# Converting 64-bit weights on the chip: nine landing places, two VectorE steps instead of three, and another order of work

## The chip, the cores and the metric

One NeuronCore of a Trainium2 chip runs the whole program. The metric is the device time of one execution in microseconds (us), lower is better. The engines are TensorE (PE, with PEld for its weight loads), VectorE (DVE), ScalarE (ACT), GpSimd (POOL) and SyncE (SP, which only issues DMAs here). Each runs its own queue of instructions strictly in order and waits on semaphores for the others.

## What is computed

A block-sparse attention over 4 batches, 8 heads, 768 positions and head size 64, followed by a feed-forward layer on its output:

```python
def _attn_ref(q, k, v, sampled_blocks):      # blocks of 32 positions, 24 blocks
    scores = scale * np.matmul(q, k.transpose(0, 1, 3, 2))
    mask = np.abs(blk_i - blk_j) <= window   # neighbours, first and last block, 3 sampled blocks
    ...
    attn = softmax(np.where(mask, scores, -1e9))
    return np.matmul(attn, v)

def _moe_ref(x, w_in, w_out):                # x (3072,512), w_in (512,2048), w_out (2048,512)
    h = x @ w_in
    g = h * np.clip(h + 3.0, 0.0, 6.0) / 6.0
    return g @ w_out
```

The weights arrive as 64-bit floats, and are made into 32-bit ones on the chip.

## The kernel before

**Tiling.** The attention is cut into 24 units, u0 to u23: a batch and a group of four blocks of queries (128 rows). Three units make a chunk of 384 rows, and each of the eight chunks goes through 16 feed-forward steps (m0 to m15 for the first chunk, m127 is the last of all). A step takes one column block of `w_in` and one row block of `w_out`: weights w0, w1 for step 0, w2, w3 for step 1 and so on to w31. Only the first chunk meets weights that are not yet on the chip as 32-bit floats. From m16 on they lie in the SBUF tiles `win` and `wout` (16 slices of 512 columns each).

**A unit.** `s` (two halves) makes the scores, `r_` (DVE, eight of them) adds the bias and takes the minimum, `e` (ACT, eight) the exponential, `t` (PE) turns them, `c` (DVE or ACT) copies them out of PSUM, `a` (PE) multiplies by the values, `n_` (DVE) divides, `x` (PE) turns the result, and `xh`, `xl` split it into a high and a low part of reduced precision. The units of a batch's group 0 (u3, u9, u15, u21) have two quarters like the others and a second part (`gs`, `gr`, `ge`, `gt`, `gc`, `ga`, ...) for the two blocks that see all keys. Values come by plain DMAs (`values`, issued by SP) and, for the sampled blocks, by indirect DMAs (`gather`, issued by POOL), into a ring `VR` of six places.

**A step.** `h` is 12 matmuls, three `o` of three matmuls each; between them ACT (`ga`, `gh`) and DVE (`gb`, and `gl` on DVE or POOL) make the activation and split it. In front of each step, `hi` (ACT) and `lo` (DVE or POOL) split the two weights. `oc` and `od` copy the result out and send it to HBM.

**A weight.** `load` brings 512 KB of raw words (low and high word of each number side by side) into a buffer `wraw`, of which there are two. `size` (ACT) scales the high word, read as a float, by 2^-112 into the weight's slice of `win` or `wout`; `bits0` (DVE) shifts that left by three; `bits1` (DVE) shifts the low word right by 29 and joins it; `bits2` (DVE) joins the sign. Then `hi` and `lo` follow. A raw buffer is free for the next load when `bits2` has read it.

**The order** is written out by hand in the table `SCORE`: a list of phrases such as `w2 size; u1 a gather0`, read from front to back, each of which records an operation (a suffix .d, .a, .p names the engine where there is a choice). Every engine's queue is this list, cut down to its own operations.

All operations are recorded by one helper, so that the profile gives them one line (L235); they are told apart by their tiles.

Of the kernel before, what the change touches and what calls it, by code (L numbers as in the profile page):

```python
# [28 lines left out]
MASKED = -8000000000.0  # L29

# [10 lines left out]
k0 load keys0; u0 q values0 values1 values2 values3; k0 clamp flag; u1 q; u0 near0.d near1.a; k0 spread; u1 values0; u0 near2.d near3.a chosen0.p; u1  # L41
values1; u0 ends0.d; w0 load; u0 ends1.d ends2.d; w1 load; u0 chosen1.p ends3.d; k0 bias number; u1 near0.d near1.a; k0 place; u0 chosen2.p; k0 rows;
u1 ends0.d ends1.d; u0 chosen3.p gather0 s0 gather1 s1 r_00 e00 r_01 e01 r_02 gather2; u2 q; u0 r_10; u1 near2.a; u0 t00 r_03 e02 gather3 r_11 e03
c00.d e10 t01; u1 chosen0.p; u0 e11 r_12; w0 size; u0 c01.d t10 e12; u1 chosen1.p; u0 r_13; w1 size; u0 c10.d e13; u1 near3.d chosen2.p; u2 near0.d
near1.a; u0 t11 d c11.a; u1 chosen3.p; w0 bits0; w1 bits0; w0 bits1; u0 a; u1 gather0; w1 bits1; u1 gather1; w0 bits2; u1 s0 values2; u0 n_; u1
values3; w0 hi; u2 chosen0.p values0; w1 bits2; u0 x; u2 values1; u1 s1; w2 load; u0 xh; u1 r_00; u2 chosen1.p; w3 load; w1 hi; w0 lo.d; u3 q; u1 e00
r_01; w1 lo.p; u1 r_10; u2 near2.a; u1 r_02 e01 gather2 r_11 e10 t00 r_03 e02 r_12 e03 gather3 c00.d e11 t01 e12 r_13 t10; u2 chosen2.p; u1 c01.d; u2
near3.a; u1 e13 c10.d; w2 size; u2 chosen3.p; u1 t11 d c11.a; u3 near2.d; u2 gather0; u3 near3.d; w3 size; u0 xl; w2 bits0; u2 gather1 s0; w3 bits0;
w2 bits1; u3 chosen2.p; u2 s1 r_00; w2 bits2; u2 e00; u1 a; u4 q; u3 chosen3.p; u2 r_01; u4 near0.a; w4 load; u2 r_10; w2 hi; u4 chosen0.p; u2 r_02
e01 values2; u1 n_; u2 e02 t00 values3; w2 lo.p; u3 values2; u2 r_03 e10; u1 x; u3 values3; u2 r_11 c00.a; w3 bits1; u2 e03; u4 near1.p; u2 e11 t01  # L50
r_12; u4 chosen1.p; u1 xh; u2 t10 c01.d; u3 s0; u2 e12 r_13 c10.a gather2; u1 xl; u2 e13; w3 bits2; w4 size; u2 t11 gather3 c11.d; w3 hi; w5 load; u2
d; u4 near2.a; u3 z0; w4 bits0; u4 near3.a; w3 lo.d; u3 gather2 r_00; w4 bits1; u3 e00 gather3; u2 a; u3 r_01; w4 bits2; u4 chosen2.p; u3 e01 r_02; w6
# [28 lines left out]
a; m13 gl.p; w27 hi; w29 load; w27 lo.d; u7 values2; u6 n_; m13 o0; u7 values3; w28 size; u8 values0; u6 x; m13 o1; w28 bits0; m13 o2; w28 bits1; u8
keys0; u7 s0; w28 bits2 hi; u7 r_00 e00 r_01; w28 lo.p; w30 load; w29 size; u7 r_02 r_03 e01; u8 values1; u7 gather2; m14 h; w29 bits0; u7 e02; w29
bits1; u7 e03 gather3; w29 bits2; m14 ga; u8 gather0; w31 load; w29 hi; m14 gb; u8 keys1; w29 lo.d; m14 gh gl.p; w30 size; m14 o0; u8 gather1; w30
bits0 bits1; m14 o1; w30 bits2; m14 o2; w30 hi; w0 hi; w30 lo.d; w0 lo.p; m15 h; w31 size bits0; m16 h; w31 bits1; m15 ga; w2 hi; m15 gb; u6 xh; w2
lo.p; w31 bits2; m15 gh; u6 xl; w31 hi; m15 gl.p; m17 h; m16 ga; w31 lo.d; w1 hi; m16 gb; w4 hi; w1 lo.p; m16 gh; m15 o0; w4 lo.d; m17 ga; u7 s1; m16
# [131 lines left out]
def fused_kernel(ctx: ExitStack, tc, qT, kN, kS, kB, vS, vB, picks, sampled, sampled_t, placing, cand, spread, w_in, w_out, ident_d, out):  # L217
# [564 lines left out]
```

## Time and profile before

| | |
|---|---|
| median of three runs | 804.61 us (802.95 to 804.74) |
| the profiled execution: time, span | 808.03 us, 806.2 us |
| PE busy | 764.5 us (95% of the span) |
| DVE, ACT, POOL busy | 508.8, 458.1, 334.1 us |
| DMA | 114.57 MB |
| mean granted TensorE clock | 0.982 |

The span runs from the program's first instruction to its last; the time has a little around it (1.8 us here). "Busy" of PE counts matmuls whose ends are modelled, so a stretch in which PE is 100% busy need not be PE at its peak. A group of instructions is told as engine, operation, what it writes <- what it reads.

### The profile page before, as it was taken

To read this page: it belongs to the slowest core of one execution; us is meant where nothing else is said; L and a number is where in the kernel's file an instruction comes from. 1 tells how busy PE (TensorE), PEld (TensorE's weight loads), DVE (VectorE), ACT (ScalarE), POOL (GpSimd) and SP (SyncE) were. 2 spreads that over 40 slices of the span, in tenths; PEclk is the share of its full clock that TensorE was granted. 3 is DMA by queue.
4 is the path that set the end of the run, shared out by engine and by line. 5 is a ranking of instruction groups with operands and counts; after the bars stand their busy time and mean duration, and the time that the engine had idled before them with its cause. 6 is when DMAs were issued, how large, how long until landed. Compare 5 with 4: busy or idle time off the path is not lost.

```text
span 806.2 us, 22075 instructions
## 1 busy us (share of the span) xinstructions
PE 764.5 (95%) x8662; PEld 635.7 (79%) x8662; DVE 508.8 (63%) x1173; ACT 458.1 (57%) x1113; POOL 334.1 (41%) x344
## 2 busy tenths in 40 slices
PE   5879888879999999999999999999999999999996
PEld 3568666658888888888888888888888788888995
DVE  5888788776556665566566764565566765555452
ACT  4674666546545766546555656556645657455453
POOL 5864363355334434445442434445443334321231
PEclk9899899999999999999999999999999999999998
DMA  8785379884123540766543540666444420311001
GB/s 307 230 253 165 119 229 322 274 297 127 30 93 93 180 139 2 244 206 188 143 134 93 170 150 2 202 203 218 139 122 122 151 91 1 120 48 39 1 1 40
DMA packets 73271, 114.57 MB, mean 142 GB/s; under 512 B 9139, under 2 KB 40759, under 8 KB 73167
## 3 DMA queue, kind: packets, MB, share of 16 engines
q1 hardware_dynamic: 65858, 89.95, 34.9%
q0 software_dynamic: 7040, 23.07, 9.3%
q8 instruction: 68, 1.11, 0.6%
q14 instruction: 37, 0.30, 0.1%
q10 hardware_dynamic: 268, 0.14, 0.1%
HBM read 106.84 MB, written 6.29 MB: 140 GB/s over the span
## 4 chain that ended last, share of the span: by engine, by line
PE 77%; DVE 1%; ACT 1%; issue 0%; DMA 0%; POOL 0%; POOLq 0%; SPq 0%; ACTq 0%
PE out L235 31%; PE h L235 30%; PE att L235 17%; DVE win L235 1%; DMA out_dram<-ot 0%; ACT p L235 0%; POOL wlo_in L235 0%; ACT whi_in L235 0%; ACT g L235 0%; DVE pt L235 0%; ACT whi_out L235 0%; ACT ot L235 0%; POOLq L778 0%; DVE wlo_out L235 0%; SPq L235 0%
## 5 line engine op out<-in xcount | busy, mean ns | idle before, releaser
L235 PE MATMUL h<-x,whi_in 128*128 128x384 f32 x1024 | 264.7, 339 | 1.6 <-ACT whi_in L235 1.6
L235 PEld LDWEIGHTS h<-x,whi_in 128*128 128x128 f32 x1024 | 186.8, 189 | 15.3 <-issue 2.9
L235 ACT ACTIVATE g<-h,half_b 128x384 f32<-128x384 f32 x128 | 74.4, 581 | 176.9 <-PE h L235 172.5
L235 PE MATMUL h<-x,wlo_in 128*128 128x384 f32 x512 | 173.1, 338 | 1.6 <-POOL wlo_in L235 1.4
L235 DVE SCALAR_TENSOR_TENSOR g<-g,h 128x384 f32<-128x384 f32 x128 | 70.7, 553 | 161.3 <-ACT g L235 160.7
L235 PE MATMUL out<-whi_out,ghi 128*128 128x512 f32 x384 | 165.7, 432 | 5.4 <-ACT ghi L235 5.2
L235 POOL TENSOR_TENSOR wlo_out<-wout,whi_out 128x512 fp32r<-128x512 f32 x60 | 78.7, 1312 | 193.6 <-ACT whi_out L235 168.8
L235 PE MATMUL out<-whi_out,glo 128*128 128x512 f32 x384 | 153.9, 401 | 2.6 <-POOL glo L235 2.0
L235 PE MATMUL out<-wlo_out,ghi 128*128 128x512 f32 x384 | 152.6, 397 | 1.5 <-POOL wlo_out L235 1.1
L235 ACT ACTIVATE p<-p,m 128x256 f32<-128x256 f32 (+1 forms) x192 | 96.2, 502 | 59.7 <-DVE m L235 59.2
L235 POOL TENSOR_TENSOR wlo_in<-win,whi_in 128x512 fp32r<-128x512 f32 x55 | 71.9, 1307 | 136.8 <-ACT whi_in L235 133.1
L235 ACT CAST whi_out<-wout 128x512 fp32r<-128x512 f32 x128 | 79.2, 619 | 49.5 <-PE out L235 44.1
L235 POOL DMA_INDIRECT vr<-vB,rows x88 | 88.4, 1004 | 32.5 <-issue 13.9
L235 POOL TENSOR_TENSOR glo<-g,ghi 128x384 fp32r<-128x384 f32 x55 | 64.8, 1179 | 88.6 <-ACT ghi L235 79.5
L235 PEld LDWEIGHTS h<-x,wlo_in 128*128 128x128 f32 x512 | 96.3, 188 | 3.7 <-POOL wlo_in L235 2.9
L235 PEld LDWEIGHTS out<-whi_out,ghi 128*128 128x128 f32 x384 | 72.7, 189 | 28.1 <-issue 10.3
L235 PEld LDWEIGHTS out<-whi_out,glo 128*128 128x128 f32 x384 | 72.7, 189 | 21.6 <-POOL glo L235 4.0
L235 ACT CAST whi_in<-win 128x512 fp32r<-128x512 f32 x128 | 78.0, 610 | 14.4 <-DVE win L235 14.4
L235 DVE TENSOR_TENSOR glo<-g,ghi 128x384 fp32r<-128x384 f32 x73 | 74.4, 1019 | 9.6 <-ACT ghi L235 9.6
L235 DVE COPY pt<-att 128x512 f32<-128x512 f32 x87 | 59.6, 688 | 33.0 <-PE att L235 32.6
L235 PEld LDWEIGHTS out<-wlo_out,ghi 128*128 128x128 f32 x384 | 73.0, 190 | 8.7 <-POOL wlo_out L235 2.3
L235 PE MATMUL att<-ident,p 128*128 128x128 f32 x452 | 69.5, 281 | 4.2 <-ACT p L235 2.1
(93 smaller groups left out, 926.9 us busy)
## 6 DMA issues: line engine op xcount, KB each, us to landing
kr<-kB SPq DMA_DIRECT2D x198, 64.0 KB
vr<-vS SPq DMA_DIRECT2D x52, 192.0 KB
vr<-vS SPq DMA_DIRECT2D x36, 256.0 KB
kr<-kS SPq DMA_DIRECT2D x48, 192.0 KB
wraw<-w_in SPq DMA_DIRECT2D x16, 512.0 KB
wraw<-w_out SPq DMA_DIRECT2D x16, 512.0 KB
kn<-kN SPq DMA_DIRECT2D x12, 512.0 KB
q<-qT SPq DMA_DIRECT2D x24, 256.0 KB
```

The costliest lines, as they stand in the source:

```text
L235: self.last = tc.keep_in_program_order(op(*a, **k)).ins
```

## The change

- Raw words land in nine places instead of two: the two `wraw` buffers (now fixed ones), the ring `ot` that the results use later, and six pairs of slices of `win` and `wout` that belong to weights of later steps. `load` gets the number of the place.
- `VR` gets six more places for the first twelve items (units u0 to u2), also in slices of `win` and `wout` that are still empty; from the thirteenth item on the ring has six places as before.
- `bits0`, `bits1`, `bits2` are replaced. `sign` (DVE, floats) multiplies the scaled word by -2^32 and takes the larger of that and the word itself. `low` turns the low word, read as an unsigned integer, into its top three bits (multiply by 2^-29, add -0.499, round to an integer), on ACT for 12 weights and on POOL for 20. `bits` (DVE) shifts left by three and joins the result of `low`.
- The table `SCORE` is a new one. It has the same number of operations (3052). Of `lo`, 180 are on DVE and 76 on POOL (141 and 115 before); of `gl`, 103 and 25 (73 and 55); of `c`, 40 on DVE and 56 on ACT (75 and 21); of `oc`, 22 and 2 (10 and 14).

```diff
+LOW = -0.499
...
+    ot_ring = const.tile([P, 2, DM], F32, name="ot")
+    landing = [sb.tile([P, 2, DM], F32, name="wraw") for _ in range(2)] + [ot_ring]
+    landing += [t[:, f:f + 2] for f in (NF - 2, NF - 4, NF - 6) for t in (win, wout)]
+    VR += [t[:, f:f + 2] for f in (4, 6, 8) for t in (win, wout)]
...
-            self.vn = len(v_items) % RING
+            n = len(v_items)
+            self.vn = n if n < 2 * RING else n % RING
...
-        def load(self):
-            self.raw = sb.tile([P, DM, 2], I32, name="wraw")
-            dma.dma_start(out=self.raw, in_=self.src.bitcast(I32).rearrange("p (n t) -> p n t", t=2))
+        def load(self, at):
+            raw = landing[at].rearrange("p a n -> p (a n)")
+            dma.dma_start(out=raw.bitcast(I32), in_=self.src.bitcast(I32))
+            self.raw = raw.rearrange("p (n t) -> p n t", t=2)
...
-        def bits(self, i):
-            low, high, wi = self.raw[:, :, 0], self.raw[:, :, 1], self.w.bitcast(I32)
-            if i == 0:
-                dve.tensor_scalar(out=wi, in0=wi, scalar1=3, scalar2=None, op0=ALU.logical_shift_left)
-            elif i == 1:
-                dve.scalar_tensor_tensor(out=wi, in0=low, scalar=29, in1=wi, op0=ALU.logical_shift_right, op1=ALU.bitwise_or)
+        def sign(self):
+            dve.scalar_tensor_tensor(out=self.w, in0=self.w, scalar=-2.0 ** 32, in1=self.w, op0=ALU.mult, op1=ALU.max)
+        def low(self, eng):
+            src, to = (self.raw[:, :, 0].bitcast(t) for t in (U32, I32))
+            if eng is act:
+                act.activation(out=to, in_=src, func=AF.Identity, scale=2.0 ** -29, bias=low_b)
             else:
-                dve.scalar_tensor_tensor(out=wi, in0=high, scalar=-0x80000000, in1=wi, op0=ALU.bitwise_and, op1=ALU.bitwise_or)
+                eng.tensor_scalar(out=to, in0=src, scalar1=2.0 ** -29, scalar2=LOW, op0=ALU.mult, op1=ALU.add)
+        def bits(self):
+            wi = self.w.bitcast(I32)
+            dve.scalar_tensor_tensor(out=wi, in0=wi, scalar=3, in1=self.raw[:, :, 0].bitcast(I32), op0=ALU.logical_shift_left, op1=ALU.bitwise_or)
...
-w0 load; u0 ends1.d ends2.d; w1 load; u0 chosen1.p ends3.d; ...
+k0 place; u0 ends1.a; w0 load0; k0 bias; ... w2 load2; u0 chosen1.p gather3 s0 ... w1 load1; ...
```

The order shows at three places. First DVE, where the first two weights are converted (`wraw` and `ot` are raw words, `p,m` the `r_` of a unit). Before:

```order
L235 TENSOR_SCALAR win_70<-win_70 128x512
L235 TENSOR_SCALAR wout_71<-wout_71 128x512
L235 SCALAR_TENSOR_TENSOR win_70<-wraw_160,win_70 128x512
L235 SCALAR_TENSOR_TENSOR wout_71<-wraw_164,wout_71 128x512
L235 SCALAR_TENSOR_TENSOR win_70<-wraw_160,win_70 128x512
L235 TENSOR_TENSOR xs_452<-h_362,den_215 128x512
L235 SCALAR_TENSOR_TENSOR wout_71<-wraw_164,wout_71 128x512
```

Now:

```order
L237 SCALAR_TENSOR_TENSOR win_70<-win_70 128x512
L237 SCALAR_TENSOR_TENSOR win_70<-win_70,wraw_105 128x512
L237 SCALAR_TENSOR_TENSOR win_70<-win_70 128x512
L237 SCALAR_TENSOR_TENSOR win_70<-win_70,ot_104 128x512
L237 ISA p_462,m_371<-h_373,bias_88 128x256
L237 ISA m_371 128x1
L237 TENSOR_TENSOR wlo_in_464<-win_70,whi_in_391 128x512
```

Two weights took six instructions (three for each) and take four; the shift of the low word is gone from this queue.

Second SP, from the loads of w0 on (`wraw`, `ot` and, where the source is `w_in` or `w_out`, `win` and `wout` are landing places; with the source `vS` these are places of `VR`). Before:

```order
L235 DMA q_260<-qT 128x512
L235 DMA vr0_79<-vS 96x512
L235 DMA vr1_80<-vS 96x512
L235 DMA vr2_81<-vS 96x512
L235 DMA vr3_82<-vS 96x512
L235 DMA wraw_495<-w_in 128x1024
L235 DMA wraw_513<-w_out 128x1024
L235 DMA q_519<-qT 128x512
L235 DMA q_726<-qT 128x512
L235 DMA wraw_742<-w_in 128x1024
```

Now:

```order
L237 DMA wraw_105<-w_in 128x1024
L237 DMA ot_104<-w_in 128x1024
L237 DMA wraw_106<-w_out 128x1024
L237 DMA q_264<-qT 128x512
L237 DMA wout_71<-w_in 128x1024
L237 DMA win_70<-w_out 128x1024
L237 DMA wout_71<-vS 128x512
L237 DMA win_70<-vS 128x512
L237 DMA wout_71<-vS 128x512
L237 DMA win_70<-vS 128x512
L237 DMA q_518<-qT 128x512
```

Five weights are asked for here before the values of u1 and u2, where two were, and these values no longer wait for a place in the old ring.

Third POOL, around the last gathers of u2 (`kr` are the chosen keys of later units). Before:

```order
L235 ISA
L235 COPY kr3_76<-kn_72 128x128
L235 DMA vr4_83<-vB,rows_89 128x512
L235 DMA vr5_84<-vB,rows_89 128x512
L235 MEMSET p_852 64x1024
L235 DMA vr0_79<-vB,rows_89 128x512
L235 DMA vr1_80<-vB,rows_89 128x512
```

Now:

```order
L237 ISA
L237 COPY kr0_73<-kn_72 128x128
L237 DMA wout_71<-vB,rows_90 128x512
L237 DMA win_70<-vB,rows_90 128x512
L237 DMA vr0_79<-vB,rows_90 128x512
L237 MEMSET p_823 64x1024
L237 DMA vr1_80<-vB,rows_90 128x512
```

The gathers of u2 went to `vr4`, `vr5`, which u1 reads until its `a` is over; they go to places that nothing else uses by then.

## Rows read from the trace of the kernel before

**Rows 1.** Windows: length, busy PE, PEld, DVE, ACT, POOL, granted clock, DMA share, GB/s
```profile
0.00:54.00 54.00, 36.25 (x691) 24.85 (x691) 39.60 (x126) 30.15 (x85) 35.58 (x81) 0.91 0.79 263
54.00:182.00 128.00, 111.68 (x1376) 85.00 (x1373) 103.09 (x230) 75.01 (x186) 58.06 (x58) 0.95 0.72 236
120.00:182.00 62.00, 51.35 (x720) 37.34 (x720) 47.80 (x107) 33.49 (x84) 26.18 (x24) 0.96 0.89 297
182.00:780.00 598.00, 597.14 (x6508) 509.24 (x6508) 358.94 (x808) 343.78 (x827) 234.78 (x203) 1.00 0.38 116
```

**Rows 2.** Chain in order of time, late stretch: start us, duration us, what
```profile
356.84 1.92 PE att L235 x128
...
783.03 2.10 PE h L235 x12
785.14 2.78 PE out L235 x12
```

**Rows 3.** Timeline of PE near 232 and 244 us: start, duration, instruction
```profile
232.57 1.09 PE L235 MATMUL att<-kr,q 64*32 64x256 f32 x32
...
243.74 0.60 PE L235 MATMUL att<-ident,p 128*128 128x128 f32 x4
244.10 0.48 PE L235 MATMUL out<-whi_out,ghi 128*128 128x512 f32 x1
```

**Rows 4.** Timeline of PE, then of POOL, 42 to 52 us
```profile
47.90 3.27 PE L235 MATMUL att<-vr,pt 128*32 128x64 f32 x114 [2.20 <-DMA vr<-vB,rows]
...
42.32 1.39 POOL L235 DMA_INDIRECT vr<-vB,rows  x1 [0.30 <-PE att L235]
```

**Rows 5.** Waits of SP's queue, 0 to 200 us: total, times, longest
```profile
SPq L235 <- DVE wout L235: 37.8, 12, 6.4
SPq L235 <- DVE win L235: 34.1, 11, 5.7
```

**Rows 6.** Groups of DVE, 0 to 190 us: count | busy, mean ns | idle before
```profile
L235 DVE SCALAR_TENSOR_TENSOR win<-wraw,win 128x512 int32<-128x512 int32 x32 | 26.1, 814 | 0.4
L235 DVE SCALAR_TENSOR_TENSOR wout<-wraw,wout 128x512 int32<-128x512 int32 x32 | 25.2, 787 | 0.4
L235 DVE CUSTOM_DVE_ANT_1 p<-att,bias 128x256 f32<-128x256 f32 x36 | 14.2, 415 | 2.2 <-PE att L235 2.1 <-PE out L235 0.2
L235 DVE COPY pt<-att 128x512 f32<-128x512 f32 x18 | 12.4, 688 | 5.0 <-PE att L235 4.8
L235 DVE TENSOR_SCALAR wout<-wout 128x512 int32<-128x512 int32 x16 | 9.5, 594 | 1.9 <-ACT wout L235 1.9
L235 DVE TENSOR_SCALAR win<-win 128x512 int32<-128x512 int32 x16 | 8.0, 499 | 1.5 <-ACT win L235 1.5
L235 DVE TENSOR_TENSOR glo<-g,ghi 128x384 fp32r<-128x384 f32 x7 | 6.7, 958 | 2.3 <-ACT ghi L235 2.3
L235 DVE TENSOR_TENSOR wlo_in<-win,whi_in 128x512 fp32r<-128x512 f32 x8 | 6.1, 767 | 2.8 <-ACT whi_in L235 2.7
```

**Rows 7.** Groups of ACT, 0 to 190 us
```profile
L235 ACT ACTIVATE p<-p,m 128x256 f32<-128x256 f32 x52 | 26.0, 502 | 16.7 <-DVE m L235 16.7
L235 ACT ACTIVATE win<-wraw 128x512 f32<-128x512 f32 x16 | 10.8, 675 | 3.5 <-DMA wraw<-w_in 3.5
```

**Rows 8.** Groups of POOL, 0 to 190 us
```profile
L235 POOL DMA_INDIRECT vr<-vB,rows x32 | 33.0, 1031 | 7.9 <-issue 6.0 <-DVE rows L235 0.5 <-PE out L235 0.3
L235 POOL TENSOR_TENSOR wlo_out<-wout,whi_out 128x512 fp32r<-128x512 f32 x12 | 16.9, 1410 | 41.1 <-ACT whi_out L235 28.1 <-issue 13.0
L235 POOL COPY kr<-kn 128x384 f32<-128x384 f32 x2 | 1.2, 597 | 0.0
```

**Rows 9.** Timeline of DVE and POOL, 83 to 88 us
```profile
83.49 0.69 DVE L235 SCALAR_TENSOR_TENSOR wout<-wraw,wout 128x512 int32<-128x512 int32 x1
...
86.84 1.36 DVE L235 SCALAR_TENSOR_TENSOR win<-wraw,win 128x512 int32<-128x512 int32 x1
...
86.34 1.31 POOL L235 TENSOR_TENSOR wlo_out<-wout,whi_out 128x512 fp32r<-128x512 f32 x1 [3.89 <-ACT whi_out L235]
```

More of the change, by code (lines that the diff above doesn't have):

```diff
@@ L40 @@
 SCORE = """
[L41 to L52, printed above, removed]
@@ L81 @@
[L81 to L84, printed above, removed]
@@ new lines @@
+near2.p; u1 values1 near1.d; k0 place; u0 ends1.a; w0 load0; k0 bias; u0 chosen3.p ends0.a; k0 rows; u1 near0.d; u0 ends2.a; u1 ends1.a; u0 chosen2.p;
+u1 ends0.a; u0 chosen0.p; w2 load2; u0 chosen1.p gather3 s0 gather2 s1 r_00 e00 r_01; w1 load1; u0 e01 r_02 gather0; u2 q; u0 r_10; u1 near2.a; u0 t00
+r_03 e02 gather1 r_11 e03; u1 near3.d; u0 e11 t01 r_12; u1 chosen3.p; u0 e10; u2 near1.d; u0 e12 t10 r_13 c00.a; w4 load4; u1 chosen2.p; u0 c01.d e13;
+u2 near0.d; u0 c10.a t11 d; u1 chosen1.p; w0 size; u0 c11.d; w0 low.a sign; u1 chosen0.p; w2 size; w0 bits; w2 low.a; w3 load3; u1 gather1; w2 sign;
@@ new lines @@
+u1 s0; w0 hi; w2 bits; w1 size; u0 a; u1 gather0; w1 low.a; u1 r_00; w0 lo.d; w2 hi; u2 chosen0.p; u1 e00 r_01 s1; w4 size; w2 lo.d; u1 values3
+values2 gather3 e01 r_02; u2 values1 values0 near3.a; u1 r_10 t00; u3 q; u1 r_03 e02 gather2; w6 load6; u1 r_11 e10; u0 n_; u1 e03; u2 near2.p; u1 e11
+r_12 t01; u0 x; u1 c00.a; u2 chosen1.p; u3 near3.d; u1 t10 r_13 e12; w5 load5; w1 sign; u1 e13; u2 chosen3.p; u1 c01.a t11 c10.d; u3 near2.a; u1
+c11.d; u2 chosen2.p; u0 xh; u1 d; w4 low.a; u0 xl; u2 gather0; w3 size; u2 s0; w1 bits; w8 load8; w3 low.a; w4 sign; u2 gather1 s1; w1 hi; u2 r_00; w1
@@ new lines @@
+lo.d; u2 e00; u1 a; u3 chosen3.p; u4 near1.a; u2 r_01; u4 near0.a; u2 r_10; u3 chosen2.p; u2 r_02 e01 r_11 e10 t00 values2; u1 n_; u2 e02 values3
+gather3; u3 values2; u2 e11 r_03; u1 x; u3 values3; u2 c00.a r_12; w7 load7; u2 gather2; w4 bits; u2 e03; u3 s0; u2 e12 r_13; u1 xh; u3 gather2; u2
+t01; w3 sign; u2 t10 e13; u1 xl; w10 load1; u2 c01.a t11; u3 z0; u2 d c10.a; w3 bits; u2 c11.a; u3 gather3; w6 size; u3 r_00 r_01 e00; u4 near2.p; w6
+sign; w3 hi; u4 near3.p; u3 e01 r_02; w9 load0; w3 lo.p; w6 low.a; u3 t00 r_03 s1 e03 c00.d e02; w5 low.p; w6 bits; w5 size; u3 z1; u5 near0.d; w8
@@ new lines @@
+h; u3 gr23 ge21; w14 bits; u3 ge31 ge32; w17 load8; w13 sign; u3 ge11; m2 o2; u3 xl ge20; w18 low.p; w13 bits; m3 o0; u3 ge30; m4 ga; u3 gt00 gd; m3
+o1; w9 hi; u3 gc00.a gt01; w9 lo.p; m4 gb; m3 o2; w12 hi; u3 gc01.d; w20 load2; u3 gt02; m4 gh; w12 lo.p; u3 gt10; m5 ga; u3 gc02.d gt11 gc10.a; m4
+gl.d; u3 ga0 gc11.a; w17 low.p; m5 gb; w11 hi; m4 o0; m5 gh; w11 lo.p; u3 gn0; w14 hi; m5 gl.d; u3 gt12; w19 load1; m4 o1; w16 size; w14 lo.d; w20
+low.p; m6 h; u3 gc12.a; w16 sign; w15 size; u4 values2; w16 bits; u4 values0; w18 size; u4 values1; w15 sign; w17 size; u3 ga1; w18 sign; m6 ga; w22
@@ new lines @@
+lo.p; u4 r_02; w24 size; m7 o1; u3 gxl; u4 e02; w24 low.p; m8 o0; u4 r_03; m9 ga; w24 sign; u4 s1 e03; u5 q; m9 gb; w22 hi; w23 low.p; w26 load4; w24
+bits; m7 o2; w23 size; u4 t00; w22 lo.p; u4 r_10; w19 hi; m8 o1; w23 sign; u4 e10; m10 h; u4 r_11; w19 lo.p; u4 c00.a; w25 load2; u5 near2.d; u4 e11
+r_12; m9 gh; u5 near3.p; w23 bits; u4 e12 t01; m9 gl.p; m10 ga; u4 r_13; m8 o2; u4 c01.a; m10 gb; u4 t10; u5 chosen2.p; u4 e13; m9 o0; u4 c10.d; m10
+gh; u4 t11 d; u5 chosen3.p; w21 hi; m9 o1; m10 gl.d; u4 c11.a; m11 h; w21 lo.d; w24 hi; w26 low.p; w28 load1; u5 values0; w26 size; w24 lo.d; u5
@@ new lines @@
+values1; w25 size low.p; w27 load0; w26 sign; u4 a; m11 ga; w25 sign; m11 gb; w26 bits; m9 o2; u5 gather2 values2; u4 n_; w26 hi; u5 values3; m10 o0;
+w25 bits; m11 gh; u4 x; w26 lo.p; w23 hi; m10 o1; m11 gl.d; w28 size; m12 h; w23 lo.d; u5 gather3; w28 low.a sign; u4 xh; w28 bits; u6 gather1; m10
+o2; w27 size; w29 load2; u4 xl; u5 s0; m12 ga; w27 low.p sign; w25 hi; m12 gb; m11 o0; u6 gather0; w28 hi; u5 r_00; m12 gh; m13 h; w25 lo.d; u5 e00;
+w28 lo.p; u5 r_01; m12 gl.d; u5 e01 r_02; u6 keys0; m11 o1; m13 ga; w27 bits; u5 s1 e02 r_03; m13 gb; u5 e03; w29 low.p; m11 o2; u5 r_10; w29 size; u5
@@ new lines @@
+t00; w30 load0; u5 r_11 e10; m12 o0; u6 q; w29 sign; w31 load1; u5 e11; m14 h; u5 r_12 c00.a; w29 bits; u5 e12; w27 hi; u5 r_13; m13 gh; w27 lo.d; u5
+t01 e13 t10 c01.d; m13 gl.p; u6 keys2; m12 o1; m14 ga; u5 c10.d t11; m12 o2; u5 d c11.a; m14 gb; m13 o0; w30 size low.p; u5 a; w29 hi; w30 sign; m14
+gh; w29 lo.d; w30 bits; m14 gl.p; m13 o1; w31 size; u6 keys3; u5 n_; u6 gather2; m14 o0; w30 hi; w31 sign; u5 x; w31 low.a; w30 lo.d; m13 o2; u6
+gather3; w0 hi; w31 bits; m14 o1; u6 keys1; u5 xh; u7 gather0; m15 h; w0 lo.d; w31 hi; u5 xl; u7 gather1; w31 lo.d; m14 o2; m15 ga; m16 h; w2 hi; m15
```

310 lines of the change are left out of this document (152 added, 158 removed).

## The prediction

> **What bounds the kernel now.** First the windows [rows 1]. From 182 to 780 us PE is busy 597 of 598 us at the full granted clock: there the other engines cost nothing (DVE 60%, ACT 57%). All that can be won lies in the first 182 us, in which the first chunk's 16 steps go through and the 32 weights are converted. I cut this stretch in two: A, 0 to 54 us, up to the first `h`; B, 54 to 182 us, up to the `h` of m15.
>
> "Busy" does not tell how much is lost there, so PE's work is priced by undisturbed rows: an `h` 2.10 us, an `o` a quarter of 2.78, 0.70, an `a` 1.92 [rows 2]; an `s` 1.09, four transposes (`t`, `gt`, `x`) 0.36 from the start of one to the next [rows 3]. `gs` counts as an `s`, a `ga` (96 matmuls to `a`'s 128) as 1.44. Counted in the table, B holds 15 `h`, 45 `o`, 10 `s` and `gs`, 24 groups of transposes, 4 `a`, 2 `ga`: 31.5 + 31.5 + 10.9 + 8.6 + 7.7 + 2.9 = 93 us of work in 128 us, 35 us lost. A holds 8 `s`, 17 groups, 3 `a`: 8.7 + 6.1 + 5.8 = 21 us in 54, 33 us lost.
>
> What ends last in B? DVE is the fullest engine, 103.1 of 128 us (80%), then ACT 75, POOL 58 [rows 1]. A step cannot start before its two weights have gone size, three bits, hi, lo, and the bits stand in DVE's queue between the units' `r_` and copies. The two landing places close a loop with it: SP waited 37.8 + 34.1 = 72 us for DVE to free them [rows 5], and behind these waits stand the values and keys of the units. From 120 to 182 us the DMA engines are 89% busy at 297 GB/s [rows 1], also near full.
>
> **The change part by part.**
>
> *Conversion on DVE.* Before, 32 weights took 26.1 + 25.2 + 9.5 + 8.0 = 68.8 us [rows 6], 0.72 for each of 96 instructions. Now there are 64 of the two-input kind. Undisturbed one takes 0.69, beside a POOL `tensor_tensor` 1.36 [rows 9]; the mean now is 0.80 [rows 6]. I take 0.75, since POOL has fewer two-input instructions in this stretch (22 instead of 29 by the table): 48 us, 21 us less over A and B. Bounds: 64 x 0.69 = 44 (none collides) and 64 x 1.02 = 65 (half of them do).
>
> [...]
>
> *`low`.* On ACT 12 times; the nearest row is `size`, 0.675 [rows 7]: 8 us. On POOL 20 times; no row shows it. From below, a one-input copy of 384 columns takes 0.60, so 512 some 0.8; from above, the two-input subtraction of 512 takes 1.41 [rows 8]. I take 0.8, nearest to a one-input operation: 16 us, with 28 as the other end. [...]
>
> *Stage A, by the new table.* PE's work is the same 21 us (one `gs` more). DVE: 16 conversions instead of 17, four copies less, three `r_` more: no change. ACT gets 4 `size`, 7 `low`, 4 `e`, 4 copies `c` and 6 small copies of keys more and 5 key copies less, about 12 us on top of 30.2: 42 of 54, the fullest now. Against it, u2 no longer waits for its values: its `a` lasted from 42.98 to 51.1, since the gather could be issued only at 42.32, after u1's `a`, and landed at 47.9 [rows 4]; with places of its own it is issued before, 6 us. What is late next is u2's last `e` and `xh` on ACT. I set the one against the other: A stays 54, between 48 (ACT hides) and 62 (8 us of ACT's 12 show).
>
> *Stage B.* The new table has 15 `h`, 44 `o`, 6 `s` and `gs`, 19 groups, 3 `a`, 2 `ga` there: 31.5 + 30.8 + 6.5 + 6.8 + 5.8 + 2.9 = 84 us of PE work, 9 less than before: u6 has moved behind m15, where PE is full, so these 9 (less the `gs` of A, 8) come back at the end. DVE in B: bits 76 to 48 instructions (54.5 to 36 us), `r_` 31 to 16 (at 0.50 with the read of its sum, -7.5), copies 13 to 5 (-5.5), `lo` 9 to 12 (+2.3), `gl` 7 to 9 (+1.9), the rest -1.4: 103.1 - 28.7 = 74 us. ACT: 16 `e` less (about -9.6), 3 `size` less, 5 `low` and 4 copies more: 70. POOL: 17 `low` (+14), 6 subtractions and 5 gathers less, 2 chosen keys more: 61. So DVE, from 10 us over PE's work, comes to 10 under it. If DVE were the bound at its present 80%, B would take 93 us; but now four engines are level (84, 74, 70, 61), each waits for the others in turn, and I take 100: PE at 84%, against 73% now. Bounds: 89 (PE at 94%) and 112.
>
> *Loads.* Nine places let SP run ahead: 12 weights are asked for before m0 instead of 7. DMA up to m0 is 2.6 MB more, 17.7 MB, which at 0.3 MB a microsecond is 59 us, but the last of these is needed only by m5. B's DMA falls from 29 to 18.5 MB, since the keys and values of u6 to u8 are asked for later. So the DMA engines leave the path in B, and are one more reason for the upper bound of A.
>
> *Behind m15* PE's work is given and at full clock; the heavier DVE (+39 `lo`, +30 `gl`, -35 copies, +12 `oc`) goes from 60% to some 64%, POOL falls. Zero, unless the rival below.
>
> **Sum.** A 0, B 100 - 128 = -28, work moved behind +8: -20 us. The profiled execution of 808.0 would become 788; the median, 804.6, becomes 784.6.
>
> **Rivals.**
> 1. *B becomes PE-bound.* POOL and DVE collide less, B 89, A 48: -39 - 6 + 8 = -37, 768 us. For it: the mean clock of 0.95 in B [rows 1] costs up to 5% of 128, 6 us, that come back if PE has no long gaps. Against: a balanced in-order pipeline never ran so full in this trace before 182 us.
> 2. *The gain goes to ACT and POOL.* The loads do run ahead but `size`, `low` and the exponentials pile up on ACT: A 62; in B `low` costs 1.4 on POOL (+12 us, 73 us) and holds up DVE: B 112. 8 - 16 + 8 = 0: 804. For it: ACT's 42 of 54 us in A; against: the whole sum in B stays under PE's work.
> 3. *Slower: the units behind m15 stall PE.* Before, some 20 us of PE work stood between a unit's first `s` and its last `t` in the steady part; in the new table it is 10.4 us (u7, u8). In these ACT has eight `e`, three `hi`, a copy and two operations of the steps, about 8 us by its rows, and can begin only when `s` and the first `r_` are through (1.09 + 0.42 [rows 3, 6]): 9.5 of 10.4. There are 18 such units. With 1.3 us of stall in each the 20 us are gone (23.4); with 2 us it is +16: 821. For it: a DVE `lo` of 1.4 instead of 0.7 in the wrong place does it. Against: the margin of 0.9 us, fewer POOL instructions to collide with, and that ACT's instructions begin some 0.1 us before the last has ended.
>
> **How the numbers follow.** Forecast 0.68, rival 1 0.10, rival 2 0.12, rival 3 0.10. The predicted time is the forecast's, 784.6; its own range, A 52 to 58 and B 92 to 108, is 775 to 797. For 8 in 10 the range reaches from 769 (rival 1, nearly) to 801 (half-way into rival 2). About 0.3% (2.4 us) is what a measurement can tell from no change: faster by more than that holds the forecast and rival 1, 0.78; within it lies most of rival 2, 0.10; slower is rival 3 and the worse part of rival 2, 0.12.
>
> **What would show it.** The `h` of m15 at about 154 us (182 now); DVE's conversions at 44 to 55 us; `low` on POOL near 0.8; SP's waits for DVE well under 72 us; u2's `a` in one piece without a wait on a gather; PE full from 160 us on. Wrong would make it: m0 later than 60 us with ACT over 85% busy (rival 2), `low` on POOL over 2.5 us (POOL would then be as full as PE in B), or gaps of PE before `t` and `a` between 200 and 780 us (rival 3).

## The result, and the profile after

The kernel takes 785.34 us (median of four runs, 783.92 to 787.4); the kernel before took 803.98 us beside it (802.95 to 804.74). The ratio is 0.977, with a 95% interval of 0.974 to 0.980: faster, by 18.6 us; 784.6 was forecast. The profiled execution has 787.4 us, its span is 785.6.

Three stretches hold the difference. Windows of after, cut where its stages now end (length, busy time of PE, PEld, DVE, ACT, POOL, granted clock, DMA share, GB/s), which answer to [rows 1]:

```profile
0.00:59.00 59.00, 37.38 (x722) 25.37 (x722) 38.58 (x125) 41.49 (x109) 41.35 (x87) 0.86 0.92 331
59.00:154.00 95.00, 91.11 (x1101) 75.41 (x1094) 87.99 (x166) 69.37 (x161) 59.55 (x64) 0.98 0.53 178
182.00:780.00 598.00, 596.49 (x6530) 509.47 (x6528) 348.08 (x850) 347.98 (x842) 156.74 (x141) 1.00 0.40 122
```

The cuts are the first `h` and the `h` of m15 in the timeline of PE (start, duration, instruction):

```profile
59.02 0.89 PE L237 MATMUL h<-x,whi_in 128*128 128x384 f32 x2
...
154.39 0.52 PE L237 MATMUL h<-x,whi_in 128*128 128x384 f32 x2
```

Stage A has grown from 54.0 to 59.0 us, stage B has shrunk from 128.3 to 95.4, and from the `h` of m15 to PE's last matmul it is 624.5 us where it was 617.5: +5.0 - 32.9 + 7.0 and 0.3 at the end make the 20.6 us between the spans (785.6 and 806.2). Look at DVE in the second row: 88 of 95 us, 93%, where B had 80%. B did not become short by a DVE with little to do, but by a DVE that hardly stops. And look at DMA in the first row: 92% at 331 GB/s, where A had 79% and 263.

Groups of DVE, 0 to 190 us (count | busy, mean ns | idle before), against [rows 6]:

```profile
L237 DVE SCALAR_TENSOR_TENSOR win<-win 128x512 f32<-128x512 f32 x16 | 16.5, 1030 | 2.2 <-ACT win L237 2.2
L237 DVE SCALAR_TENSOR_TENSOR wout<-wout 128x512 f32<-128x512 f32 x16 | 13.6, 851 | 0.1
L237 DVE SCALAR_TENSOR_TENSOR win<-win,wraw 128x512 int32<-128x512 int32 x6 | 4.9, 819 | 0.2
L237 DVE SCALAR_TENSOR_TENSOR wout<-wout,wraw 128x512 int32<-128x512 int32 x6 | 4.2, 704 | 0.0
```

The first two are the 32 `sign`. With the 32 `bits` (of which two rows stand here) the 64 instructions of the conversion take 55.7 us of DVE, 0.87 each, where the 96 of before took 68.8, 0.72 each. Of POOL and ACT, against [rows 7, 8], two of the rows of `low`:

```profile
L237 POOL TENSOR_SCALAR wraw<-wraw 128x512 int32<-128x512 uint32 x7 | 5.6, 798 | 0.6
L237 POOL TENSOR_SCALAR ot<-ot 128x512 int32<-128x512 uint32 x4 | 3.7, 922 | 0.3
```

```profile
L237 ACT ACTIVATE wraw<-wraw,low_b 128x512 int32<-128x512 uint32 x5 | 3.9, 773 | 0.0
```

Waits of SP's queue, 0 to 200 us, against [rows 5]; DVE is still what it waits for (`wout` and `win`: 67.7 us in 12 waits, where it was 71.9 in 23), with loads that are further ahead:

```profile
SPq L237 <- DVE wout L237: 57.8, 10, 9.4
SPq L237 <- PE att L237: 41.1, 5, 10.0
SPq L237 <- DVE win L237: 9.9, 2, 5.4
```

What PE itself waits for in B tells more. Waits of PE over B, first of before (54 to 182.3 us), then of after (59 to 154.4 us):

```profile
PE out L235 <- ACT ghi L235: 5.2, 4, 2.1
PE out L235 <- POOL glo L235: 1.6, 3, 0.9
PE h L235 <- ACT whi_in L235: 1.6, 2, 1.4
```

```profile
PE out L237 <- ACT whi_out L237: 1.6, 1, 1.6
PE att L237 <- issue: 1.0, 1, 1.0
PE out L237 <- POOL wlo_out L237: 0.8, 1, 0.8
```

The longest waits of before, those of an `o` for its activation (`ghi`, `glo`), are gone; all listed waits together fall from some 16 to 4 us. That is 12 of the 24 us by which the time above PE's priced work has shrunk (35 to 11). The rest stands in no listed wait: it lies in PE's busy time, which was 111.8 us for 93 us of priced work and is 91.5 for 84.5. The granted clock, 0.95 before and 0.98 now, has at most some 4 us of it (an estimate: 5% of 128 less 2% of 95).

### The profile page after: what moved, and what is told of

It reads as the page before. It is cut to its first block, busy times and chain, and to the rows that moved or that the text cites. A ratio compares the mean times of both kernels' runs of the same rounds, so it can differ in the third digit from the quotient of the medians.

```text
span 785.6 us, 21998 instructions
## 1 busy us (share of the span) xinstructions
PE 753.0 (96%) x8662; PEld 634.4 (81%) x8662; DVE 493.4 (63%) x1183; ACT 474.8 (60%) x1148; POOL 267.6 (34%) x300
## 4 chain that ended last, share of the span: by engine, by line
PE 80%; DVE 1%; issue 0%; DMA 0%; ACT 0%; SPq 0%; DVEq 0%
PE out L237 32%; PE h L237 30%; PE att L237 18%; DMA out_dram<-ot 0%; DVE ot L237 0%; DVE p L237 0%; DVE glo L237 0%; DVE win L237 0%; DVE g L237 0%; DVE wout L237 0%; SPq L237 0%; DVE pt L237 0%; DVE x L237 0%; ACT g L237 0%; DVE wlo_out L237 0%
## 5 line engine op out<-in xcount | busy, mean ns | idle before, releaser
L237 PE MATMUL out<-whi_out,glo 128*128 128x512 f32 x384 | 151.8, 395 | 0.0
L237 POOL DMA_INDIRECT vr<-vB,rows x82 | 85.1, 1037 | 111.5 <-PE att L237 94.7
L237 POOL TENSOR_TENSOR wlo_in<-win,whi_in 128x512 fp32r<-128x512 f32 x42 | 55.0, 1310 | 149.1 <-ACT whi_in L237 72.5
L237 DVE TENSOR_TENSOR wlo_out<-wout,whi_out 128x512 fp32r<-128x512 f32 x94 | 67.7, 720 | 31.2 <-ACT whi_out L237 30.4
L237 POOL TENSOR_TENSOR wlo_out<-wout,whi_out 128x512 fp32r<-128x512 f32 x34 | 43.8, 1289 | 120.4 <-ACT whi_out L237 87.7
L237 DVE TENSOR_TENSOR glo<-g,ghi 128x384 fp32r<-128x384 f32 x103 | 65.0, 631 | 20.8 <-ACT ghi L237 20.6
L237 ACT CAST ghi<-g 128x384 fp32r<-128x384 f32 x128 | 65.2, 510 | 14.2 <-PE out L237 7.1
L237 DVE CUSTOM_DVE_ANT_1 p<-att,bias 128x256 f32<-128x256 f32 (+1 forms) x176 | 67.6, 420 | 8.1 <-PE att L237 7.5
```

The costliest lines, as they stand in the source:

```text
L237: self.last = tc.keep_in_program_order(op(*a, **k)).ins
```

## Experiments

The time of the kernel before is not the same on every chip (804.0, 814.8, 810.4 and 805.0 us, median, beside the four sets of runs), so a ratio is always to the kernel before on the same chip. "m0" and "m15" are the starts of their `h` in PE's timeline, B is what lies between, and the last two columns are DVE's busy time and the granted clock in B from the windows. These stages come from one profiled execution each: for the kernel before they are 54.0 and 128.3 us on one chip, 57.6 and 124.5 on another, so some 4 us between two rows tell little.

| kernel | ratio to before (95%) | m0 | m15 | B | DVE in B | clock in B |
|---|---|---|---|---|---|---|
| before, with the result | 1 | 54.0 | 182.3 | 128.3 | 103.1 | 0.95 |
| after, with the result | 0.977 (0.974-0.980) | 59.0 | 154.4 | 95.4 | 88.4 | 0.98 |
| e1_places | 1.006 (1.004-1.008) | 62.1 | 191.0 | 128.9 | 103.6 | 0.97 |
| e2_conversion | 1.005 (1.003-1.007) | 57.0 | 185.8 | 128.8 | 93.5 | 0.97 |
| e5_oldorder | 1.013 (1.010-1.016) | 62.2 | 190.8 | 128.6 | 92.7 | 0.97 |
| e3_oldconv | 0.982 (0.980-0.984) | 60.9 | 158.1 | 97.2 | 92.6 | 0.98 |
| b_before, second set | 0.999 (0.997-1.001) | 57.6 | 182.1 | 124.5 | 104.9 | 0.99 |
| e7_deep | 1.020 (1.016-1.025) | 55.0 | 188.8 | 133.8 | 102.9 | 0.96 |
| e9_units | 1.012 (1.008-1.017) | 57.9 | 180.0 | 122.1 | 98.7 | 0.97 |
| e10_unitsdeep | 1.032 (1.026-1.037) | 57.7 | 192.6 | 134.9 | 97.4 | 0.88 |
| g1_lead | 1.019 (1.016-1.021) | 56.2 | 195.2 | 139.0 | 105.9 | 0.93 |
| g2_leadconv | 1.011 (1.009-1.013) | 54.5 | 187.8 | 133.3 | 95.0 | 0.94 |
| g3_cut | 0.985 (0.983-0.987) | 54.0 | 159.5 | 105.5 | 81.8 | 1.00 |
| g4_five | 0.974 (0.972-0.977) | 54.9 | 149.7 | 94.8 | 88.5 | 1.00 |

### First set: the three parts of the change, alone and together

The change has three parts: places, conversion, table. The forecast's theory is that DVE's load, and with it the conversion, decides B; the rivals are the places and the table. The table of before with the places alone (and the old three steps), with the conversion alone (two landing places, six for values), and with both; and the new table with the places and the old three steps:

```diff
 e1_places, e5_oldorder: the table of before
-... w2 load; u0 xh; ... w9 load; ...
+... w2 load2; u0 xh; ... w9 load0; ...
 e2_conversion, e5_oldorder
-w6 size; ... w6 bits0; ... w6 bits1; ... w6 bits2; ... w6 hi
+w6 size low.a; ... w6 sign; ... w6 bits; ... w6 hi
 e3_oldconv: the new table
-... w6 size; u3 r_00 ...; w6 sign; ... w6 low.a; ... w6 bits; ...
+... w6 size; u3 r_00 ...; w6 bits0 bits1; ... w6 bits2; ...
```

> The table of before, its three VectorE steps, but nine landing places and the twelve places for values (the loads stand where they stood; each takes the place that has been free longest). SP's 72 us of waits for VectorE should nearly vanish and the weights land early. If VectorE's work is what bounds stage B (the forecast's theory), the time hardly moves: 800 to 806 us, h of m15 at 178 to 184 us. If the landing places were the bound, B shrinks by 15 us or more: under 790 us, h of m15 near 165.

> The table of before with two landing places and six places for values, and the new conversion alone: sign stands where bits0 stood, bits where bits2 stood, bits1 is gone, low stands behind size, on ACT for the same 12 weights as in the new kernel and on POOL for 20. VectorE's conversions 68.8 -> about 52 us. If VectorE's work is the bound of B, this brings a good part of the 20 us: 788 to 796, h of m15 at 166 to 174 us. If the landing places were the bound, SP still waits some 70 us for VectorE and the time stays at 800 to 806; the three engines in a row per weight (ACT, POOL, VectorE) may then even hold a place longer than before: up to 810.

> The table of before with both parts: nine landing places, twelve places for values and the new conversion. If conversion and places do it all, about 785 to 790 us. If the order of work is what brings the gain (u6 behind m15, fewer r_ and copies of units in B on VectorE), this stays near the better of the two single changes, 790 to 800.

> The new kernel with the old three steps: low is left out, bits0 and bits1 stand where sign stands, bits2 where bits stands; nine places and the new table. VectorE, 88 of 95 us busy in B of the new kernel, gets about 24 steps of 0.65 us there more (16 us) and ACT and POOL lose low (20 us together). If VectorE is the bound of B: 794 to 800 us, h of m15 at 164 to 170. If the new table and the places bring the gain and VectorE's load does not matter: 784 to 788.

In the old table nothing of the change gains: places +0.6%, conversion +0.5%, both +1.3%. B stays at 128.6 to 128.9 us in all three, whether DVE works 103.6 us in it or 92.7. (The new conversion also gives POOL 16 us and ACT 4 us more, but what PE waits for POOL in B hardly grows, from 3.4 us in e1_places to 3.9 in e5_oldorder.) With the places A is 62 us, without them 57. In the new table, with the old conversion, B is 97.2 and the time 1.8% under before: nearer to what the table alone was to give (784 to 788 us beside 804, 0.975 to 0.980) than to a bound by DVE (794 to 800, 0.988 to 0.995). Windows over B of e1_places, e5_oldorder and e3_oldconv, all on one chip:

```profile
62.10:191.00 128.90, 109.56 (x1376) 84.25 (x1374) 103.58 (x231) 75.28 (x187) 58.20 (x58) 0.97 0.66 221
```

```profile
62.20:190.80 128.60, 109.31 (x1377) 83.74 (x1375) 92.74 (x206) 78.98 (x193) 74.27 (x77) 0.97 0.66 222
```

```profile
60.90:158.10 97.20, 92.06 (x1102) 75.72 (x1095) 92.56 (x189) 65.70 (x155) 43.84 (x44) 0.98 0.52 172
```

These rows decide it. From the first to the second DVE loses 11 us and B nothing; in the last two DVE's busy time in B is the same, 92.7 and 92.6 us, and B differs by 31 us, of which 9 are PE work that the new table does later. e2_conversion was to be 1 to 2% under before and is 0.5% over it; e5_oldorder was to be 785 to 800 us beside 804 and is 1.3% over. So neither DVE's load nor the places bounded B in the old table; the table did. (The new table was not run with two places; five are the least that were tried, below.) In the new table DVE is busy for 95% of B in e3_oldconv and 93% in after, and there the conversion seems to pay: 0.982 to 0.977, some 3.6 us, but the intervals just touch and come from two chips, so that this gain is not shown.

### Second set: two properties of the new table, put into the old one

What does the table do? Counted in PE work (each operation at the price of the prediction's rows), three things differ in steps m3 to m15. Between an `h` and its `o0` stand 0 to 4 us in the old table from m4 to m14, 6 to 12 in the new one. Between the last bits step of a weight of `w_in` and the `h` that needs it stand 2.0 us on average in the old, 12.0 in the new. And u6 has gone behind m15. The first and the third were put into the kernel before, each alone and both together, with the kernel before itself beside them:

```diff
 e7_deep (and e10_unitsdeep), the o of m3 to m14
-... w9 lo.p; m4 gl.d; w10 bits2; m4 o0; u3 gr11; ... m4 o1; u3 gr12; m4 o2; u3 gr13; w11 size; m5 h; ... u3 gs2; m5 ga; ...
+... w9 lo.p; m4 gl.d; w10 bits2; u3 gr11; ... u3 gr12 gr13; w11 size; m5 h; ... u3 gs2; m4 o0; m5 ga; ... m4 o1; ... m4 o2; ...
 e9_units (and e10_unitsdeep), from m15 on the new table, u6 and u7 with it
-... w23 hi lo.d; m11 h; u6 gather0 r_00 e00 ...
+... m15 oc0.d; ... m16 o0; u6 e00 r_01; ...
```

> The kernel before, unchanged, so that its stages can be read on the same chip as those of the three beside it. Every theory: ratio 1.000, m0 at about 54 us, B (h of m0 to h of m15) 128 us.

> The kernel before, where alone the three o of steps 3 to 14 stand later in the table: between the end of an h and its step's o0 there are now 4.2 to 8.4 us of other TensorE work instead of 0 to 4.1 (2.0 on average for steps 4 to 14; in the new table 5.8 to 12.3). Theory S (the new table gains because two steps are in flight, so that TensorE does not stand before an activation that is not done): B 128 -> 112 to 118, ratio 0.980 to 0.988. Rival U (the gain comes from having fewer units' work in B) and rival V (VectorE's work is the bound): B 126 to 130, ratio 0.997 to 1.003.

> The kernel before (old conversion, two landing places) with its own order for u0 to u5, the steps up to m14 and the first conversion of the weights, and the new table's order for everything else: u6 and u7 go behind m15, and all behind m15 is in the new order. Rival U: B 128 -> 105 or less, ratio 0.975 to 0.985. Theory S: B loses u6's and half of u7's TensorE work (9 us) and little more, B 115 to 119, and the work comes back later: ratio 0.994 to 1.002. Rival V: VectorE's work in B falls by some 10 us, B 115: ratio 0.994 to 1.002, too.

> Both edits: u6 and later in the new order, and the o of steps 3 to 14 later (4.2 to 8.3 us of work between an h and its o0). If these two are what the new table brings, this comes to where the new table with the old conversion came: B 95 to 102, ratio 0.980 to 0.985 (a little lower, if stage A stays at 54 us). If the fine order of the conversions in B is needed too: B over 106, ratio 0.987 to 0.995.

All three are slower, and no theory had that. Waits of PE in e7_deep, 111 to 189 us (m8 to m15; total, times, longest):

```profile
PE h L235 <- ACT whi_in L235: 12.0, 5, 4.3
PE att L235 <- DVE m L235: 3.0, 1, 3.0
PE h L235 <- POOL wlo_in L235: 2.2, 3, 0.9
```

The waits of `o` for the activation are gone, as meant. In their place each `h` stands before `whi_in`, the high part of its weight: 12.0 us, where b_before has 1.4 in its steps m8 to m15 (110 to 182 us). What ACT, which makes the high parts, waits for shows in b_before, 110 to 182 us:

```profile
ACT whi_in L235 <- DVE win L235: 10.8, 5, 3.1
ACT p L235 <- DVE m L235: 7.3, 7, 2.0
...
ACT whi_out L235 <- DVE wout L235: 4.1, 2, 2.1
```

`hi` waits 10.8 + 4.1 us for the last bits step on DVE: each weight is finished just before its use. The `o` had covered this. The edit itself takes part of the cover away: with the `o` moved behind, the PE work between the last bits step and the `h` falls from 2.0 to 1.5 us on average, and there is none before six `h`, where there was none before two. So e7_deep did not change the first property alone. With u6 away (e9_units) B falls by 2.4 us only, though 7.0 us of PE work have left it, and the work comes back later: from the `h` of m15 to PE's last matmul it takes 631.0 us where b_before takes 620.8. Alone, moving u6 is a loss. In e10_unitsdeep a part of the 134.9 us is clock: 0.88 was granted in B, where e9_units had 0.97.

### Third set: how far ahead the weights are made

So the second property was tried, both ways. Into the old table: weights earlier, with the old and with the new conversion. Out of the new one: weights later. In g1_lead the last bits step of w25, for one, stands 11 us of PE work ahead of m12's `o0` instead of 1.1; in g3_cut that of w8 stands 0.7 us ahead of m4's `h` instead of 19.5. And the new kernel with five landing places.

```diff
 g1_lead, g2_leadconv: the table of before, w6 to w31
-... m12 gb; w25 hi; u5 xl; m12 gh; w25 lo.p; ...
+... w25 bits2; ... w25 hi; ... w25 lo.p; ... m12 gb; u5 xl; m12 gh; ...
 g3_cut: the new table, w6 to w31
-... u2 x; w8 bits; u3 gs0; ... m0 h; ... m0 o0; w8 hi; ... w8 lo.d; u3 gr11; ... m2 o0; ... m4 h; ...
+... u2 xh; ... m0 h; ... m0 o0; ... u3 gr11; ... m3 h; w7 low.p size; w8 bits; ... w8 hi; ... w8 lo.d; ... m2 o0; m3 ga; m4 h; ...
 g4_five: the new table
-... w8 load8; ... w7 load7; ... w10 load1; ...
+... w1 bits; w8 load2; ... w4 bits; w7 load3; ... w3 bits; w10 load4; ...
```

> The table of before with the old conversion; units, steps and the distance from h to o stay where they stood. Moved are only the weights w6 to w31: load, size and the three bits steps stand earlier by an amount that grows through B, and hi and lo about 3 us of TensorE work earlier where their two buffers allow it. So the last bits step stands 8.2 us of TensorE work ahead of the h that needs the weight, instead of 2.0, and lo 3.3 instead of 0.9 (in the new table 12.0 and 4.8). Such a table needs more than two landing places; it has nine from w6 on. Theory L (B was long because each weight was finished just in time, so that every delay in the chain bits, hi, lo stopped TensorE): B 128 -> 110 to 118, ratio 0.980 to 0.990. Rival: the place of the conversions does not matter (nothing else in the old order gives way): B 126 to 130, ratio 0.997 to 1.006.

> The same earlier weights with the new conversion (sign, low, bits; low behind size on the engines of the new kernel). Theory L: with the lead there VectorE's load is what is left, and a third of the conversion less now pays: 3 to 8 us under the run with the old conversion, ratio 0.972 to 0.986. If the conversion costs time in the old order whatever the lead (as it did without the lead, +0.5%): ratio as with the old conversion or up to 0.5% above it.

> The new kernel with the lead taken away: for w6 to w31 size, low, sign and bits stand later, hi and lo too, so that bits stands 1.5 us of TensorE work ahead of its use (12 in the new table) and lo 0.6 us (4.8); eight loads stand later, as their places are read later. Two VectorE steps, the engines, nine places, u6 behind m15 and the distance from h to o (5.8 to 12.3 us) are those of the new kernel. Theory L: B 95 -> 112 to 125, ratio to the kernel before 0.997 to 1.015. Rival V (VectorE's load and the places bring the gain): the ratio stays at 0.977 to 0.982.

> The new kernel with five landing places instead of nine; loads stand where they stood, or behind the last read of their place, whichever is later. Five is the least that lets nearly all steps of the conversion stand where they stand. In A the loads of w8, w7 and w10 wait for w1, w4 and w3, so that 1.5 MB less is asked for between 29 and 36 us. Theory D (A became longer, m0 at 59 us, because weights fill the DMA engines, 92% busy, while TensorE's instructions and the gathers of u1 and u2 come through the same engines): u1's a without its 3.5 us stop, m0 at 54 to 57, ratio 0.970 to 0.976. If the early loads are harmless: m0 at 59, ratio 0.976 to 0.980. If all nine places are needed in B: B over 99 us, ratio over 0.980.

g1_lead misses: it is 1.9% slower, B 139. Its waits of ACT, then of PE, 116 to 196 us, tell why:

```profile
ACT p L235 <- DVE m L235: 21.9, 11, 4.6
ACT g L235 <- PE h L235: 7.0, 1, 7.0
```

```profile
PE out L235 <- ACT ghi L235: 4.4, 4, 2.5
PE att L235 <- DVE x L235: 2.7, 1, 2.7
PE att L235 <- DVE pt L235: 2.3, 2, 1.6
```

The waits of `hi` for DVE, 14.9 us in b_before, have vanished from the list. But the exponentials (`p`) now wait 21.9 us for the `r_` of their unit, 7.3 before: the conversions that went forward stand in front of the `r_` in DVE's queue, and PE waits for the units and for the activations (`ghi`), which ACT makes between the exponentials, instead of the weights. In the old table one wait is only traded for the other. (The granted clock in B, 0.93, adds to the 139 us.) g2_leadconv, with a third fewer DVE steps, gets 0.75% of that back (6 us, B 133.3): the new conversion pays here by the 3 to 8 us that were expected, though at 1.011 the ratio misses its range too.

g3_cut, the new table without the lead, is at 0.985: between the two ranges expected, 0.997 to 1.015 if the lead were all and 0.977 to 0.982 if it were nothing. Its window over B and its waits of PE there:

```profile
54.00:159.50 105.50, 93.91 (x1103) 73.68 (x1096) 81.82 (x165) 69.63 (x161) 62.03 (x59) 1.00 0.51 165
```

```profile
PE h L236 <- POOL wlo_in L236: 4.8, 7, 1.2
PE out L236 <- POOL wlo_out L236: 2.6, 4, 0.9
```

B grows by 10 us (11 against g4_five, on the same chip), with DVE at 81.8 us: as many DVE instructions in B, less DVE time, and B still longer. PE waits for the parts of the weights, as theory L says. Against that A is 54.0 us, 5 shorter: the conversions of w6 and w8 on DVE no longer lie in it, and some loads also go out later (that of w3 at 21.8 us instead of 16.0), so which of the two it is stays open. The lead is thus worth 10 us of B. What makes up the rest, from 105.5 to the 124.5 or 128.3 of before, is partly the 9 us of work that went behind m15; the other 10 to 14 us are left for all else that differs, the distance of `o`, the order of DVE's queue, and the conversion and the places in that order. These were not tried apart: a table of before with weights ahead and `o` late at once was not run.

g4_five is at 0.974 (after: 0.977, on another chip; the intervals overlap, so a gain over nine places is not shown). B is 94.8: five places do for this table, the other four bring nothing that these runs can tell. m0 comes at 54.9, as theory D expected; but u1's `a` still stops for 1.2 us, and g3_cut with its nine places has m0 at 54.0 on this chip, so theory D is not shown.

## Why the prediction came out right, and where its reasons were not

- **The sum.** Forecast: A 0, B -28, work moved +8, together -20. Measured: A +5.0, B -32.9, behind m15 +7.0, end +0.3. The total is right to a microsecond by luck, because A and B erred against each other.
- **What bounds B.** The reading that 35 us were lost in B, that behind m15 there is nothing to win, and that 80% of DVE makes it the fullest engine, holds. The step from there ("If DVE were the bound at its present 80%, B would take 93") failed as an explanation: e5_oldorder takes 11 us off DVE in B against e1_places and B does not move. 80% busy was the sign of queues that waited for each other, not of a load. The prediction said of the balanced engines that "each waits for the others in turn", and took from the table only counts; the order in it, which the diff shows in full, was the main thing. Its distances (`h` to `o0`, bits to `h`) could have been counted beforehand. (In its count of B one group of transposes is missing, before and after alike: 25 and 20, not 24 and 19. The difference stands.)
- **DVE's conversions.** 48 forecast, 55.7 measured, inside 44 to 65. In B, DVE did not fall to 74 us but to 88.4. The conversions there are 48 at 0.92, not 0.75 (44.2 us instead of 36), and `lo` 13 instead of the 12 counted, at 0.91. POOL has fewer two-input subtractions, and still 13 two-input DVE instructions of B lie over 1.15 us, 14 us more than at 0.69 each; before there were 9, with 7 us. Each of these 22 overlaps a POOL subtraction; up to 190 us in after, the 13 conversions that overlap one take 1.44 on average, the other 51 take 0.73.
- **`low`.** On POOL 16.5 us, 16 forecast; on ACT 9.4, 8 forecast. Eleven of the 64 `sign` and `bits` overlap a `low` on POOL. Two of these also meet a POOL subtraction (1.50 and 1.53); the other nine take 0.68 to 1.14, together 1.5 us more than at 0.69 each. So of the hold-up of DVE by `low`, which the second rival assumes, this case shows some 3 us at most, the two counted in.
- **POOL and ACT in B.** 61 and 70 forecast, 59.6 and 69.4 in the window. These sums of counts by rows came out.
- **Stage A.** 54 forecast, 59.0 measured, inside 48 to 62. u2's `a` is in one piece, without its 8 us, as forecast (52.2 to 55.8). ACT has 41.5 us, 42 forecast. What seems to have failed is the step of the loads. The prediction itself put 17.7 MB at 59 us and then took it for harmless ("the last of these is needed only by m5"); by rows 1 its own sum is 16.8 MB (54 us at 263 GB/s, and 2.6), and measured are 19.5 (59 us at 331). For it: the places alone make A 62 us where the same table without them has 57 (e1_places and e5_oldorder against e2_conversion, one chip). g4_five and g3_cut have A 4 to 5 us shorter than after, but on another chip, and the kernel before itself has 54.0 and 57.6 on two chips. The clock is part of it, and the prediction left it out of A: it is 0.86 in A, 0.91 before. u2's `a` took 3.6 us instead of 1.92 at a granted clock of 0.50 (row below, 52.2 to 55.5 us); the clock had been at 0.50 from 38.5 to 45.3, too, and fell to it, from 0.99, while PE stood in u1's `a` (36.4 to 39.9, last section).

```profile
52.20:55.50 3.30, 3.30 (x132) 3.30 (x128) 3.10 (x8) 2.97 (x8) 3.24 (x8) 0.50 0.75 290
```

- **SP's waits.** "Well under 72 us" for DVE did not come: 67.7 for `wout` and `win`. SP runs further ahead and waits there; B shrank all the same.
- **Rivals.** The first (B 89, A 48) came half-way in B alone; of its 6 us for the clock at most 4 came back in B. The second had its sign, m0 near 60 us, but ACT at 70% and B far below 112. Of the third nothing is seen: PE is busy 596.5 of 598 us behind 182, and after m15 the time above PE's priced work is 18.7 us (19.4 before).

## What to carry to other kernels

An engine at 80% in a stretch where all queues are in order need not be its bound: before its work is made cheaper, count how much work of the stalled engine stands between a result and its use in the written order. In the old table a cheaper step, more buffers, more distance or more lead each did harm alone; the traces of two of them (distance, lead) show one wait traded for the next. Together, in an order written for them, they paid. The new order with the new buffers also had the DMA engines busier early on (92% in A, 79% before; the places alone, in e1_places, had 73% up to 54 us); what else needs them then is to be looked at, though no run here parts its cost from the rest.

## What the runs showed of the hardware that was not expected

**TensorE stopped without a semaphore, at a fixed place in its program, and went on 1.3 to 1.6 us after a packet of instructions had landed.** u1's `a` in after, timeline of PE, and the DMA queues from 37 to 38.6 us (packets, MB, share):

```profile
36.22 0.22 PE L237 MATMUL att<-win,pt 128*32 128x64 f32 x1
39.90 0.27 PE L237 MATMUL att<-wout,pt 128*32 128x64 f32 x1 [3.46 <-issue]
```

```profile
q0 software_dynamic: 87, 0.30, 60.6%
q1 hardware_dynamic: 105, 0.19, 39.3%
q8 instruction: 1, 0.02, 4.6%
```

The matmul at 39.90 has no semaphore to wait for ("issue"); its `pt` was written by 33.7, and matmuls before it had read the same values. In this window one packet of instructions, 16 KB, comes in on a queue of its own, from 37.27 to 38.46, and 1.4 us later PE goes on. The same matmul stops in every kernel with this table: packet landed and PE on again at 40.31 and 41.81 (e3_oldconv), 35.09 and 36.51 (g3_cut), 35.75 and 37.01 (g4_five, a stop of 1.2 us); in e5_oldorder another `a` does so at 28.99 and 30.54. An `a` is 128 matmuls and 128 weight loads in 1.92 us. Over the span of after this queue brings 68 packets of 16 KB, and PE has 17,324 matmuls and weight loads: 255 to a packet, an estimate that gives all these packets to PE, so that an `a` uses up about one of them. In all four kernels the stop comes after the same 473 matmuls, 961 records of PE's queue, and that in e5_oldorder after 449 records, 512 fewer, about two packets by the same estimate. That the load of the DMA engines (92% in A) is the cause is not shown: the packet itself took 0.97 to 1.24 us in these five, and no run changes the load alone.

**One two-input DVE instruction took 4.72 us beside three POOL subtractions, where undisturbed ones take 0.69.** DVE, then POOL, in after, near 105 us:

```profile
104.61 4.72 DVE L237 SCALAR_TENSOR_TENSOR win<-win 128x512 f32<-128x512 f32 x1
109.25 0.54 DVE L237 SCALAR_TENSOR_TENSOR g<-g,h 128x384 f32<-128x384 f32 x1
```

```profile
104.98 1.30 POOL L237 TENSOR_TENSOR wlo_out<-wout,whi_out 128x512 fp32r<-128x512 f32 x1
106.22 2.55 POOL L237 TENSOR_TENSOR wlo_in<-win,whi_in 128x512 fp32r<-128x512 f32 x2
```

ACT, then PE, right behind:

```profile
109.88 0.51 ACT L237 CAST ghi<-g 128x384 fp32r<-128x384 f32 x1 [3.09 <-DVE g L237]
```

```profile
111.93 0.51 PE L237 MATMUL out<-whi_out,ghi 128*128 128x512 f32 x1 [1.55 <-ACT whi_out L237]
114.27 2.27 PE L237 MATMUL att<-kr,q 64*32 64x256 f32 x32
```

One `sign` took 4.72 us instead of 0.69, over three POOL subtractions back to back (3.8 us), and 4.71 at the same place in g4_five. [rows 9] had shown 1.36 beside one. ACT stood 3.09 us for the `g` that DVE made next, and PE's longest wait in B of after, 1.55 us before the `o0` at 111.93, is for the cast of `whi_out` that stands behind it on ACT. The `s` at 114.27 took 2.27 us instead of 1.09: from 113.6 to 117.0 us, after that wait and one of 0.85 us, a clock of 0.50 was granted. That all this comes from the one `sign` was not tried; g4_five has the same 4.71 us, a granted clock of 1.00 in B, and B of 94.8 us.
